# Attention with a routed expert layer in one kernel: the first weight split a step earlier, counts for the second token list later, one transposition and one small load moved

## The chip, the cores and the metric

The kernel runs on one core of a Trainium2 chip. The metric is device time in microseconds (us) of one execution; lower is better. Engines have short names here: PE is TensorE (matmuls; PEld its weight loads), DVE VectorE, ACT ScalarE, POOL GpSimd, SP SyncE, whose queue issues most DMAs. Each engine works through its own instructions strictly in the order in which the program was written.

## What is computed

Attention over 8 batches, 8 heads, 576 positions, width 64, in which keys and values are first condensed into 32 memory rows by a softmax over `phi`; its 4608 x 512 result goes through a layer of 8 experts, of which each token takes one.

```python
a = softmax(phi, over the 32 memory rows)
k_m = einsum('bhsm,bhsd->bhmd', a, k);  v_m = einsum('bhsm,bhsd->bhmd', a, v)
attn = softmax(q @ k_m^T / 8)
x = (attn @ v_m)                      # as 4608 tokens x 512
e = argmax(x @ w_gate)                # one expert for each token
gate = softmax(x @ w_gate)[e];  eom = sigmoid(x @ w_output_gate)[e]
out = gate * eom * (relu(x @ w1[e]) @ w2[e])
```

## The kernel before

**Attention.** The 8 batches are worked in 4 pairs (`NBP`). For a pair, `memory` turns the softmaxed `phi` (`turn_a`), sums keys and values into memory rows (`sums`), scales them (`spread`), turns `k_m` for use as weights (`turn_kv`) and multiplies `v_m` with both gate matrices, the tile `wg` (`gates`, copied by `gates2`). The order of these small steps is the tuple `MEM` (first pair: `MEM0`), in which "." gives control back. A pair has five steps `t` of the main loop `attention`; each runs through the list `ORDER`: `C` makes scores, `S` subtracts the largest, `X` takes exponentials, `D` and `B` divide and transpose, `V0` and `V1` multiply with the values, `M` and `m` advance `memory`, `R` advances the routing. The attended rows are stored to `xs` in DRAM.

**Routing.** After each pair, `rank` finds each token's expert and place. Token lists are made three times: list a behind the second pair and list b behind the third (both `route_early`), and list l behind the last (`route_late`). Each starts with `counts`, one matmul on `ohc` into the PSUM tile `pr`, and ends with index tiles `idx_...`, by which POOL gathers token rows (`xg`).

**Experts.** The work is cut into slots of 1 to 3 blocks of 128 tokens of one expert; two slots take list a, three take list b, the others list l. A slot has 8 weight units of 128 x 1024. Each comes by a DMA on SP's queue (`w`, buffers of the ring `raw`) and is split into a high and a low part: a cast on ACT and a subtraction on DVE into a tile `whl` of the ring `ring`. The first four units give 24 matmuls each (L1176), the last four 18 (L1198, three blocks). `turn_x` transposes the next slot's tokens on PE (L1041) while the present one runs.

**How the two meet.** The main loop runs alone up to item `S` of step `START` = 17, where it yields "open". From there on the expert code leads: `hook` is called every 6 or 12 expert matmuls and advances the attention loop by three items and the routing by two. `hold(n)` lets a routing step wait until `n` items have passed, but only once "open" has been yielded. `split(2)` under item `W` splits the first two weight units; `grow` at the end of step 16 adds buffers to `raw` and `ring` in the space that the attention inputs used.

Of the kernel before, what the change touches and what calls it, by code (L numbers as in the profile page):

```python
# [17 lines left out]
B, H, S, D, M = 8, 8, 576, 64, 32  # L18
# [14 lines left out]
NSLOT = NPE + NPT + NPP + NSS  # L33
NTHR = 13

ORDER = ["R4", "W", "X", "S", "R0", "m", "D", "M", "B", "V0", "R1", "R1", "V1", "M", "m", "C"]
LAG = {"X": 1, "B": 2, "D": 1, "V": 3, "C": -1}
TICK = 0
HOOK = (3, 2)
START = 17  # L40
# [3 lines left out]
NRAW = 3  # L44
NRING = 2
NLD = 2
MEM = ("a8", "a0", ".", "a2", ".", ".", "s0", ".", "a4", "s2", "x", "x", ".", ".", "s8", ".", "p0", "a6", ".", "x", ".", "s4", "x", "t0", ".", ".", "s9", "g0", "v0", ".", "s6", ".", "x", ".", "p1", "x", "t1", ".", ".", ".", "g1", "v1", ".")
MEM0 = ("a0", "s0", ".", "a2", "a8", ".", "s2", ".", "s8", "p0", "a4", ".", ".", "t0", ".", "g0", "a6", ".", "v0", "s9", "s4", ".", "s6", ".", ".", "p1", ".", "t1", "x", "x", ".", "g1", "x", ".", "v1", "x", ".", "x", ".", "x", ".", ".")
AWP = 1
NPK = 1  # L50
# [2 lines left out]
LATE = {"lg": 8, "w": 2, "pe": 3, "dve": 2}  # L53
# [13 lines left out]
def attention_moe(tc, phiT, kv, qT, wgo, wall, out):  # L67
    nc = tc.nc
    V, A, G, T = nc.vector, nc.scalar, nc.gpsimd, nc.tensor

    with contextlib.ExitStack() as ctx:
# [84 lines left out]
        G.affine_select(out=upto[:], in_=upto[:], pattern=[[1, E], [-1, E]], base=0,  # L156
                        channel_multiplier=0, compare_op=ALU.is_ge, fill=0.0)
        wg = cp.tile([P, H, 16], F32, name="wg")
        nc.sync.dma_start(wg[64:128], wgo)

        ohg = rt.tile([P, NCHT, E], BF16, name="ohg", bufs=1)
        jg = rt.tile([P, NCHT], I32, name="jg", bufs=1)
# [118 lines left out]
        def route_early(k):  # L281

            nm, n, s0, nch = "ab"[k], NPS[k], sum(NPS[:k]), (k + 2) * NCH
            eo, en = epcs[k], epcs[k + 1]
            yield from take_pr()
            yield from hold(LATE["pe"])
            n_ = counts(k + 1)
            yield
            yield from hold(LATE["dve"])
            fi = rt.tile([P, 1, E], F32, name="fi")  # L290
            ge = triples(fi[:, 0], n_, thr_e)
            next(ge)
            taken.clear()
            yield
            yield from ge
            V.scalar_tensor_tensor(fi[:, 0], fi[:, 0], 3.0, eo[:], ALU.mult, ALU.subtract)
            yield
            inc = (yield from prefix(fi[:], 1))[:, 0]
            exc = rt.tile([P, E], F32, name="exc")
            ie = rt.tile([P, E], F32, name="ie")  # L300
            V.tensor_scalar(ie[:], inc, 3.0 * n, None, ALU.min)
            V.tensor_tensor(exc[:], inc, fi[:, 0], ALU.subtract)
            yield
            V.tensor_scalar(exc[:], exc[:], 3.0 * n, None, ALU.min)
            cle = count_le(slot[:, s0:s0 + n], iota_3[:, 0:n], n, ie[:])
            next(cle)
            yield
            next(cle)
            V.tensor_tensor(ie[:], ie[:], exc[:], ALU.subtract)
            yield  # L310
            last(cle)
            V.tensor_tensor(en[:], eo[:], ie[:], ALU.add)
            V.tensor_tensor(exc[:], exc[:], eo[:], ALU.subtract)
            known(*order[s0:s0 + n])
            yield
            if k == 0:
                yield from hold(LATE["w"])
                stream.fetch()
            t1, t2, t3 = yield from lookup(nch, exc[:], en[:], eo[:])
            while k + 1 not in ranked:  # L320
                yield
            j = jg[:, 0:nch]
            V.scalar_tensor_tensor(t1, t1, 1.0, j, ALU.add, ALU.add)
            V.tensor_tensor(t2, j, t2, ALU.is_lt)
            V.tensor_tensor(t3, j, t3, ALU.is_ge)
            yield
            V.tensor_tensor(t1, t1, t2, ALU.mult)
            yield
            V.tensor_tensor(t1, t1, t3, ALU.mult)
            yield  # L330
            yield from table(nm, t1, nch, 3 * n)
            for z in order[s0:s0 + n]:
                z["listed"] = True
            if k == 0:
                gathers(0)
            yield
# [125 lines left out]
        def hold(n):  # L462

            if "open" not in env:
                return
            end = clock[0] + n
            while clock[0] < end:
                yield
# [115 lines left out]
        stream = Stream(0, NPE + NPT + NPP)  # L584
# [42 lines left out]
        def load_phi(bp):  # L627
            ph = ld.tile([P, 4, S], F32, name="ph")
            src = phiT[bp].rearrange("p (x s) -> p x s", s=S)
            for i in ((0, 2, 1, 3) if bp == 0 else (None,)):  # L630
                if i is None:
                    nc.sync.dma_start(ph[:], src)
                else:
                    nc.sync.dma_start(ph[:, i], src[:, i])
            phs[bp] = ph
# [14 lines left out]
        def loads():  # L650

            load_phi(0)
            for bp in range(NBP):
                for c in (0, 2, 4, 6):
                    load_kv(bp, c)
                    load_kv(bp, c + 1)
                    if bp == 0 and c == 2:
                        load_kv(0, 8)
                        load_q(0)
                        load_q(1)  # L660
                    if bp == 0 and c == PHI1:
                        load_phi(1)
                    if bp == 0 and c == 6:
                        for n in range(2, NQ):
                            load_q(n)
                    yield
# [399 lines left out]
        def attention():  # L1066

            nonlocal rou
            st, lgs = {}, {}
            while 0 not in kTs:  # L1070
                mem.step()
            st[0] = scores(0, 0)
            load_q(NQ)
            xo = None
            for t in range(NT + LAG["V"]):
                for w in ORDER:
                    g = t - LAG.get(w[0], 0)
                    if w in ("M", "m"):
                        if w == "M" or t % 5 < 4:
                            mem.step()  # L1080
                    elif w[0] == "R":

                        if len(left) < NBP - 1:
                            rou.step(int(w[1:]) * (2 if len(left) == 2 else 1))
                    elif w == "W":

                        while t == START and stream.split(2):
                            pass
                    elif w == "V0" and 0 <= g < NT:
                        bp, c = g // 5, g % 5  # L1090
                        while 2 * bp + (c >= 2) not in ves:
                            mem.step()
                        if g == 5 * bp:
                            lgs[bp] = rt.tile([P, NCH, 16], F32, name="lg", bufs=2)
                        xo = wk.tile([P, 2, 2, 2 * XQ], F32, name="xo", bufs=2)
                        values(bp, 2 * c, st[g], xo)
                    elif w == "V1" and 0 <= g < NT:
                        if c < 4:
                            values(bp, 2 * c + 1, st[g], xo)
                        store(bp, c, xo, lgs[bp])  # L1100
                    elif w == "C" and 0 < g < NT:
                        while 2 * (g // 5) + (g % 5 >= 2) not in kTs:
                            mem.step()
                        st[g] = scores(g // 5, g % 5)
                        if g + NQ < NT:
                            load_q(g + NQ)
                    elif w == "S" and 0 <= g < NT:
                        shift(st[g])
                    elif w == "X" and 0 <= g < NT:
                        expo(st[g])  # L1110
                    elif w == "D" and 0 <= g < NT:
                        divide(st[g])
                    elif w == "B" and 0 <= g < NT:
                        back(st[g])
                    undefer()
                    clock[0] += 1
                    yield "open" if w == "S" and t == START else None
                g = t - LAG["V"]
                if g >= 0 and g % 5 == 4:
                    bp = g // 5  # L1120
                    undefer(99)
                    left.append(bp)
                    rou.finish()
                    if bp < NBP - 1:
                        rou = Side(rank(bp, lgs[bp]))
                    else:
                        late.gens.append(rank(bp, lgs[bp]))
                if t == START - 1:
                    mem.finish()
                    pl.close()  # L1130
                    grow(0)
                if t == NT - 2:
                    pm.close()
# [232 lines left out]
```

## Time and profile before

| | |
|---|---|
| three runs | 577.61, 578.09, 582.82 us; median 578.09 us |
| the profiled execution | 577.36 us, of which the span of its instructions is 575.6 us |
| PE busy | 529.1 us, 92% of the span |
| DVE, ACT, POOL busy | 356.1, 280.4, 229.2 us |
| mean granted PE clock | 0.966 of full speed |

The times of rows count from the span's start. A timeline row is: start, duration, engine, line and operation, output<-inputs, shape, how many were merged, and in brackets the idle time of the engine just before with what ended it. The clock that PE was granted is given as a share of full speed: 1.00 is 2.4 GHz and 0.50 is 1.2 GHz.

### The profile page before, as it was taken

Reading aid. Unit: us, or ns where it says so; the run is one execution under the profiler, and the core shown is the slowest. Engines: PE = TensorE matmul, PEld = TensorE weight load, DVE = VectorE, ACT = ScalarE, POOL = GpSimd, SP = SyncE. Lnnn points to the kernel's source line nnn. Section 1 sums busy time; section 2 is a strip of 40 time slices with the busy share of each in tenths; the row PEclk is TensorE's granted clock in tenths of the full one; section 3 lists DMA queues with packets and bytes.
Section 4 is the critical chain, followed back from the end, with each engine's and each line's share of the span. In section 5 each row is a group of like instructions: output and inputs, shape, how many; then the busy total and the mean of one; then the engine's idle time right before and its main releaser. Section 6 shows DMA issues by size and latency. Waiting matters only on the chain. (4 is left out here: it accounts for less than half of the span.)

```text
span 575.6 us, 10886 instructions
## 1 busy us (share of the span) xinstructions
PE 529.1 (92%) x4031; PEld 455.6 (79%) x4031; DVE 356.1 (62%) x736; ACT 280.4 (49%) x496; POOL 229.2 (40%) x253
## 2 busy tenths in 40 slices
PE   3688886789899999999999999999999999999993
PEld 2455554478689799898998989898998989899893
DVE  4485979767765659996443555646465555676610
ACT  3475655454254456453434545445454445656510
POOL 2242575831166034312471735547170604553011
PEclk9987879989899999999999999999999999999998
DMA  8999999975367659756564665656465655687000
GB/s 308 413 401 391 382 376 356 308 301 168 116 197 245 209 173 308 246 155 183 161 200 145 204 177 180 184 171 176 139 202 168 179 172 181 198 264 223 7 28 32
DMA packets 42238, 124.14 MB, mean 216 GB/s; under 512 B 10368, under 2 KB 10432, under 8 KB 41792
## 3 DMA queue, kind: packets, MB, share of 16 engines
q1 hardware_dynamic: 35136, 102.71, 54.7%
q0 software_dynamic: 7040, 20.65, 10.4%
q8 instruction: 33, 0.54, 0.4%
q14 instruction: 29, 0.24, 0.1%
HBM read 102.99 MB, written 20.87 MB: 215 GB/s over the span
## 5 line engine op out<-in xcount | busy, mean ns | idle before, releaser
L1176 PE MATMUL bps<-xh,whl 128*128 128x384 f32 (+1 forms) x896 | 213.6, 322 | 0.1
L1198 PE MATMUL bps<-whl,hh 128*128 128x512 f32 x608 | 197.7, 396 | 0.0
L565 DVE TENSOR_TENSOR whl<-w,whl 128x1024 fp32r<-128x1024 f32 x112 | 136.8, 1228 | 68.5 <-ACT whl L564 68.5
L1176 PEld LDWEIGHTS bps<-xh,whl 128*128 128x128 f32 x896 | 156.9, 190 | 1.9 <-issue 0.6
L1176 PE MATMUL bps<-xl,whl 128*128 128x384 f32 (+1 forms) x448 | 143.8, 321 | 0.0
L1198 PEld LDWEIGHTS bps<-whl,hh 128*128 128x128 f32 x608 | 114.7, 189 | 26.1 <-issue 2.5
L1198 PE MATMUL bps<-whl,hl 128*128 128x512 f32 x304 | 119.0, 391 | 0.0
L564 ACT CAST whl<-w 128x1024 fp32r<-128x1024 f32 x112 | 116.4, 1046 | 0.0
L519 POOL DMA_INDIRECT xg<-xs,idx_ql x80 | 90.2, 1127 | 25.2 <-issue 24.3
L1181 ACT ACTIVATE hh<-bps 128x384 fp32r<-128x384 f32 (+1 forms) x96 | 48.9, 510 | 96.9 <-PE bps L1176 96.7
L1182 DVE SCALAR_TENSOR_TENSOR hl<-bps,hh 128x384 fp32r<-128x384 f32 (+1 forms) x96 | 55.1, 577 | 52.1 <-ACT hh L1181 52.1
L1176 PEld LDWEIGHTS bps<-xl,whl 128*128 128x128 f32 x448 | 85.1, 190 | 0.5
L1156 POOL DMA_INDIRECT out<-y,idx_ol x23 | 24.9, 1081 | 127.1 <-ACT y L1155 101.4
L1198 PEld LDWEIGHTS bps<-whl,hl 128*128 128x128 f32 x304 | 57.5, 189 | 10.8
L838 POOL TENSOR_TENSOR ea<-ea,mx 128x512 f32<-128x512 f32 (+1 forms) x20 | 19.2, 961 | 49.8 <-DVE mx L836 45.4
L1043 ACT CAST xh<-xt 128x384 fp32r<-128x384 f32 (+1 forms) x32 | 14.7, 460 | 37.9 <-DVE xt L1035 37.9
L873 ACT COPY xo<-bpd 128x576 f32<-128x576 f32 x36 | 22.6, 640 | 21.3 <-PE bpd L871 12.7
L956 POOL TENSOR_SCALAR Aw<-iota_row,row 128x128 bf16<-128x128 bf16 x36 | 26.8, 759 | 12.4 <-DVE row L946 12.4
L871 PE MATMUL bpd<-ve_b,aT 64*128 64x144 f32 (+1 forms) x320 | 28.5, 327 | 2.4 <-DVE ea L833 2.4
L1044 DVE TENSOR_TENSOR xl<-xt,xh 128x384 fp32r<-128x384 f32 (+1 forms) x32 | 15.8, 492 | 24.1 <-ACT xh L1043 24.1
L1155 ACT ACTIVATE y<-bps,gx 128x512 f32<-128x512 f32 x20 | 13.4, 687 | 30.4 <-PE bps L1198 13.9
L871 PEld LDWEIGHTS bpd<-ve_b,aT 64*128 64x128 f32 (+1 forms) x320 | 21.7, 196 | 8.1 <-issue 3.5
(248 smaller groups left out, 471.6 us busy)
## 6 DMA issues: line engine op xcount, KB each, us to landing
w<-wall SPq DMA_DIRECT2D x112, 512.0 KB, 3.9
kvt<-kv SPq DMA_DIRECT2D x32, 512.0 KB, 7.5
xs<-xo SPq DMA_DIRECT2D x16, 576.0 KB, 5.8
qt<-qT SPq DMA_DIRECT2D x16, 512.0 KB, 9.1
ph<-phiT SPq DMA_DIRECT2D x3, 1152.0 KB, 12.1
kv<-kv SPq DMA_DIRECT2D x4, 512.0 KB, 9.0
xg<-xs,idx_ql POOLq DMA_INDIRECT x80, 4.2
ph<-phiT SPq DMA_DIRECT2D x4, 288.0 KB, 3.2
```

Of the source, the lines that this page charges most:

```text
L519: G.indirect_dma_start(out=z["xg"][:, k, XQ * b:XQ * b + XQ], out_offset=None, in_=xs[0:z["rows"]].rearrange("t (a q) -> (t a) q", a=4), i ...
L564: A.copy(hl[:, 0], w[:])
L565: V.tensor_tensor(hl[:, 1], w[:], hl[:, 0].bitcast(F32), ALU.subtract)
L838: G.tensor_tensor(eav, eav, mx[:, 0:n].unsqueeze(2).to_broadcast([P, n, M]), ALU.subtract)
L871: T.matmul(px[to:to + n, r, sl], z["aT"][h, o:o + n], ves[2 * bp + b][h, g], start=True, stop=True)
L873: A.copy(xo[:, c % 2], px[:, :, 0:2 * XQ])
L956: (G if AWP else V).tensor_scalar(Aw[:, bp * NCH + c], iota_row[:], row[:, c:c + 1], None, ALU.is_equal)
L1156: G.indirect_dma_start(out=out, out_offset=bass.IndirectOffsetOnAxis(ap=z["idx"][1][:, z["q0"] + k:z["q0"] + k + 1], axis=0), in_=y[:], in ...
L1176: T.matmul(pb[:, j % pb.shape[1], 0:n_], w[:, b, o:o + P], x[a][:, cc, 0:n_], start=(n == 0), stop=(n == 11))
L1181: A.activation(h_[:, js, 0:n_], pb[:, :, 0:n_], AF.Relu)
L1182: V.scalar_tensor_tensor(l_[:, js, 0:n_], pb[:, :, 0:n_], 0.0, h_[:, js, 0:n_].bitcast(F32), ALU.max, ALU.subtract)
L1198: T.matmul(py[k], h[u - 4][a][:, f, k * P:(k + 1) * P], w[:, b, DM * f:DM * f + DM], start=(u == 4 and f == 0 and n == 0), stop=(u == 7 an ...
```

## The change

Four edits: item `W` leaves its place ahead of `X` for one between the last `M` and `m`, and its condition asks for step 16 instead of 17; in `MEM` the second turning of `k_m` ("t1") trades places with the pause behind it; `route_early` holds 6 items instead of 3 ahead of its counts; the load of `wg` is issued behind the four loads of the first `phi` instead of ahead of them.

```diff
-ORDER = ["R4", "W", "X", "S", "R0", "m", "D", "M", "B", "V0", "R1", "R1", "V1", "M", "m", "C"]
+ORDER = ["R4", "X", "S", "R0", "m", "D", "M", "B", "V0", "R1", "R1", "V1", "M", "W", "m", "C"]
...
-MEM = (... "p1", "x", "t1", ".", ".", ".", "g1", "v1", ".")
+MEM = (... "p1", "x", ".", "t1", ".", ".", "g1", "v1", ".")
...
         wg = cp.tile([P, H, 16], F32, name="wg")
-        nc.sync.dma_start(wg[64:128], wgo)
...
             yield from take_pr()
-            yield from hold(LATE["pe"])
+            yield from hold(2 * LATE["pe"])
             n_ = counts(k + 1)
...
             load_phi(0)
+            nc.sync.dma_start(wg[64:128], wgo)
             for bp in range(NBP):
...
                     elif w == "W":
-                        while t == START and stream.split(2):
+                        while t == START - 1 and stream.split(2):
                             pass
```

The edit of `MEM` moves no instruction on any engine: nothing else is written between its old and its new place. The other three do. Behind the edited lines, line numbers of the changed kernel are smaller by one.

**The counts for list b, on PE and on DVE.** On PE, during the first slot, before:

```order
L871 MATMUL bpd<-ve_b,aT 128x144 x4
L278 LDWEIGHTS ones_b
L278 MATMUL pr<-ohc_91,ones_b 128x8
L1198 MATMUL bps<-whl,hh 128x512
L1198 MATMUL bps<-whl,hl 128x512
L1198 MATMUL bps<-whl,hh 128x512 x2
L1198 MATMUL bps<-whl,hl 128x512
L1198 MATMUL bps<-whl,hh 128x512
L825 MATMUL bpd<-qt,kT_203 32x64 x8
L825 MATMUL bpd<-qt,kT_204 32x64 x8
L1041 MATMUL bps<-ident,xg 128x128 x3
```

The same stretch of PE in the changed kernel:

```order
L871 MATMUL bpd<-ve_b,aT 128x144 x4
L1198 MATMUL bps<-whl,hh 128x512
L1198 MATMUL bps<-whl,hl 128x512
L1198 MATMUL bps<-whl,hh 128x512 x2
L1198 MATMUL bps<-whl,hl 128x512
L1198 MATMUL bps<-whl,hh 128x512
L825 MATMUL bpd<-qt,kT_202 32x64 x8
L825 MATMUL bpd<-qt,kT_203 32x64 x8
L277 LDWEIGHTS ones_b
L277 MATMUL pr<-ohc_91,ones_b 128x8
L1041 MATMUL bps<-ident,xg 128x128 x3
```

The counts now stand behind six expert matmuls and the sixteen score matmuls. On DVE, the producer of `ohc` and the first reader of the counts (L192, in the changed kernel L191), before:

```order
L913 TENSOR_TENSOR ohc_91<-ohc_90,oc 128x8
L916 TENSOR_REDUCE zs<-w__2080 128x9
L192 TENSOR_TENSOR tge<-pr,thr_e 128x104
L194 TENSOR_REDUCE fi<-tge 128x8
L1044 TENSOR_TENSOR xl<-bps,xh 128x384
L833 STREAM_TRANSPOSE ea<-bpd 128x256
L836 TENSOR_REDUCE mx<-ea 128x8
L990 TENSOR_REDUCE lg<-xo 128x32
```

And in the changed kernel:

```order
L913 TENSOR_TENSOR ohc_91<-ohc_90,oc 128x8
L916 TENSOR_REDUCE zs<-w__2080 128x9
L1044 TENSOR_TENSOR xl<-bps,xh 128x384
L833 STREAM_TRANSPOSE ea<-bpd 128x256
L836 TENSOR_REDUCE mx<-ea 128x8
L990 TENSOR_REDUCE lg<-xo 128x32
L191 TENSOR_TENSOR tge<-pr,thr_e 128x104
L193 TENSOR_REDUCE fi<-tge 128x8
```

The writer of `ohc` keeps its place; the reader of the counts now stands behind four operations of attention and expert work.

**The first two splits, on DVE at the end of the attention part.** Before:

```order
L852 RECIPROCAL sa<-sa 128x16
L858 STREAM_TRANSPOSE aT<-ea 128x256
L779 COPY ve_b<-bpa 128x2x16
L565 TENSOR_TENSOR whl<-w,whl 128x1024 x2
L833 STREAM_TRANSPOSE ea<-bpd 128x512
```

And in the changed kernel:

```order
L852 RECIPROCAL sa<-sa 128x16
L858 STREAM_TRANSPOSE aT<-ea 128x256
L564 TENSOR_TENSOR whl<-w,whl 128x1024 x2
L779 COPY ve_b<-bpa 128x2x16
L833 STREAM_TRANSPOSE ea<-bpd 128x512
```

The two subtractions now stand ahead of one small copy; on ACT the two casts keep their place among the same neighbours.

**The index tiles of list b, on DVE during the second slot.** Before:

```order
L990 TENSOR_REDUCE lg<-xo 128x32
L242 CAST hl_i<-pr 128x2x9
L244 SCALAR_TENSOR_TENSOR iv<-hl_i 128x9
L1182 SCALAR_TENSOR_TENSOR hl<-bps,hh 128x384
L858 STREAM_TRANSPOSE aT<-ea 128x256
L249 TENSOR_SCALAR idx_gb<-iv 128x9
L250 TENSOR_SCALAR i_2548<-iv 128x9
L252 SCALAR_TENSOR_TENSOR idx_ob<-iv,i_2548 128x9
```

And in the changed kernel:

```order
L990 TENSOR_REDUCE lg<-xo 128x32
L1182 SCALAR_TENSOR_TENSOR hl<-bps,hh 128x384
L858 STREAM_TRANSPOSE aT<-ea 128x256
L241 CAST hl_i<-pr 128x2x9
L243 SCALAR_TENSOR_TENSOR iv<-hl_i 128x9
L1182 SCALAR_TENSOR_TENSOR hl<-bps,hh 128x384
L564 TENSOR_TENSOR whl<-w,whl 128x1024
L248 TENSOR_SCALAR idx_gb<-iv 128x9
L249 TENSOR_SCALAR i_2567<-iv 128x9
L251 SCALAR_TENSOR_TENSOR idx_ob<-iv,i_2567 128x9
```

The indices come one L1182 and one weight subtraction later than before.

## Rows read from the trace of the kernel before

**Rows 1.** The page's part 2, the span in 40 slices of 14.4 us

```profile
PE   3688886789899999999999999999999999999993
PEclk9987879989899999999999999999999999999998
DMA  8999999975367659756564665656465655687000
```

**Rows 2.** Waits of PE from 85 to 170 us: total us, times, longest

```profile
PE pr L278 <- DVE ohc L913: 3.9, 2, 2.4
```

**Rows 3.** Timeline from the start, SP's queue and DVE

```profile
0.80 0.59 SPq L159 DMA_DIRECT2D wg<-wgo  x1
...
1.44 1.99 SPq L634 DMA_DIRECT2D ph<-phiT  x4
...
6.45 2.67 DVE L677 TENSOR_REDUCE nmx<-ph 128x1 f32<-128x576 f32 x4
```

**Rows 4.** Timeline at the first splits

```profile
114.68 0.19 DVE L779 COPY ve_b<-bpa 128x32 f32<-128x32 f32 x1 [0.95 <-PE bpa L774]
...
115.93 2.36 DVE L565 TENSOR_TENSOR whl<-w,whl 128x1024 fp32r<-128x1024 f32 x2 [1.05 <-ACT whl L564]
...
118.20 0.71 DVE L833 STREAM_TRANSPOSE ea<-bpd 128x512 f32<-128x512 f32 x1
...
118.97 1.41 PE L1041 MATMUL bps<-ident,xg 128*128 128x128 f32 x9 [1.87 <-DVE ea L833]
```

**Rows 5.** Timeline around the counts for list b

```profile
142.55 0.76 PE L871 MATMUL bpd<-ve_b,aT 64*128 64x144 f32 x8
...
145.46 0.16 DVE L913 TENSOR_TENSOR ohc<-ohc,oc 128x8 bf16<-128x8 bf16 x1
...
145.68 0.17 PE L278 MATMUL pr<-ohc,ones_b 128*128 128x8 bf16 x1 [2.37 <-DVE ohc L913]
...
145.70 0.47 PE L1198 MATMUL bps<-whl,hh 128*128 128x512 f32 x1
...
145.88 0.27 DVE L192 TENSOR_TENSOR tge<-pr,thr_e 128x104 f32<-128x104 f32 x1
...
147.32 0.68 PE L825 MATMUL bpd<-qt,kT 64*32 64x64 f32 x32
...
147.93 0.90 PE L1041 MATMUL bps<-ident,xg 128*128 128x128 f32 x3
...
149.38 0.56 DVE L1044 TENSOR_TENSOR xl<-bps,xh 128x384 fp32r<-128x384 f32 x1 [2.94 <-ACT xh L1043]
...
150.66 0.37 DVE L990 TENSOR_REDUCE lg<-xo 128x32 f32<-128x128 f32 x1
...
150.90 0.21 PE L924 MATMUL pr<-ohg,strict 128*128 128x72 bf16 x1
```

**Rows 6.** Windows: stretch, its length, busy of each engine, granted PE clock, DMA share, GB/s

```profile
114.00:116.00 2.00, 2.00 (x38) 0.73 (x34) 0.27 (x2) 2.00 (x4) 0.55 (x1) 0.50 1.02 408
...
147.00:148.00 1.00, 1.00 (x35) 0.51 (x34) 0.00 (x0) 0.00 (x0) 0.00 (x0) 0.57 0.40 94
148.00:149.00 1.00, 1.00 (x4) 0.96 (x5) 0.00 (x0) 0.13 (x1) 0.00 (x0) 0.50 0.87 317
...
150.00:151.00 1.00, 1.00 (x7) 0.64 (x6) 0.97 (x4) 0.91 (x1) 0.11 (x1) 0.72 0.54 212
```

**Rows 7.** Timeline from list b to the transpositions for the third slot

```profile
177.57 0.17 DVE L252 SCALAR_TENSOR_TENSOR idx_ob<-iv,i 128x9 int32<-128x9 f32 x1
...
178.96 1.23 DVE L565 TENSOR_TENSOR whl<-w,whl 128x1024 fp32r<-128x1024 f32 x1 [0.38 <-ACT whl L564]
...
181.38 1.00 POOL L525 DMA_INDIRECT xg<-xs,idx_gb  x1 [0.30 <-issue]
...
191.04 0.49 PE L1041 MATMUL bps<-ident,xg 128*128 128x128 f32 x3
```

**Rows 8.** Gathers by lists a and b (L525) from 100 to 200 us

```profile
DMA to landing us min/median/max: 3.8/6.0/8.1
```

More of the change, by code (lines that the diff above doesn't have):

```diff
@@ L46 @@
 NLD = 2
-MEM = ("a8", "a0", ".", "a2", ".", ".", "s0", ".", "a4", "s2", "x", "x", ".", ".", "s8", ".", "p0", "a6", ".", "x", ".", "s4", "x", "t0", ".", ".", "s9", "g0", "v0", ".", "s6", ".", "x", ".", "p1", "x", "t1", ".", ".", ".", "g1", "v1", ".")
+MEM = ("a8", "a0", ".", "a2", ".", ".", "s0", ".", "a4", "s2", "x", "x", ".", ".", "s8", ".", "p0", "a6", ".", "x", ".", "s4", "x", "t0", ".", ".", "s9", "g0", "v0", ".", "s6", ".", "x", ".", "p1", "x", ".", "t1", ".", ".", "g1", "v1", ".")
 MEM0 = ("a0", "s0", ".", "a2", "a8", ".", "s2", ".", "s8", "p0", "a4", ".", ".", "t0", ".", "g0", "a6", ".", "v0", "s9", "s4", ".", "s6", ".", ".", "p1", ".", "t1", "x", "x", ".", "g1", "x", ".", "v1", "x", ".", "x", ".", "x", ".", ".")
```

## The prediction

> **What bounds the kernel now.** I read the page's slices first, by row: they split the span in two. Up to about 115 us the DMA engines stand at 9 in every slice but the first, and PE between 3 and 8; from about 160 us PE stands at 9 to the end of its work [rows 1]. So the first part is set by how early its bytes are moved, the second by PE alone, and a change can only pay where the loads begin, where one part hands over to the other, or where PE still waits behind that. The digits show such a place: the eleventh slice of PE, 144 to 158 us, is lower than those around it, though expert work is under way. The list of PE's waits names the cause: the counts matmul L278 waits for DVE's `ohc` [rows 2], and of its two waits the longer, 2.37 us, stands in the timeline at 145.68 [rows 5]. The windows show what follows: right behind the wait the clock of PE falls to about half, 0.57, 0.50 and 0.72 of full speed from 147 on (the window from 149 reads as the one from 148) [rows 6]. After 160 us there is nothing for this change to win, as PE never stands still; there the question is only what it may spoil.
>
> **The counts behind six expert matmuls.** The PE timeline [rows 5] gives the sum. PE is free at 142.55 + 0.76 = 143.31 and stands until 145.68. In the changed order it first does the six L1198, which took 145.70 to 147.32 = 1.62 us, and the scores L825, 147.32 to 147.93 = 0.61 us: 143.31 + 1.62 + 0.61 = 145.54. Its counts then need `ohc`, which DVE finishes at 145.46 + 0.16 = 145.62, since nothing ahead of L913 on DVE has changed. So they run at about 145.7 still, with a wait of 0.1 to 0.2 us, and the transpositions L1041 start at about 145.9 instead of 147.93: 2.0 us.
>
> Then the clock. From 147.93 to 150.90 PE did the three transpositions (0.90 us) and six L1198 at a lowered clock. At full speed the six take the 1.62 us seen above, and half of 0.90 is 0.45: 2.07 in place of 2.97, another 0.9 us. That the clock stays up is my reading of the rows: it was also at 0.50 at 114 us [rows 6], behind the slices in which PE is at 6 and 7, and its digits are 9 throughout where PE's are [rows 1]. If the wait goes and the clock with it, this edit is worth 2.9 us. Upwards it is bounded by the whole wait and the whole shortfall of the clock in those four windows: 2.37 + 0.43 + 0.50 + 0.50 + 0.28 = 4.1 us. Downwards by nothing gained, if the wait appears elsewhere.
>
> The Trainium skill (TensorE: Matmul & The Clock Gate, Part 1: The HAM clock gate) says that what watches PE's activity runs free of the kernel, so that the same kernel meets the change of clock at other matmuls in other runs. By that the 0.9 us would be a property of this one execution, and the edit would be worth 2.0 us.
>
> What is next late? Three places. First L924, which needs the PSUM tile that L192 has read, and L192 now stands behind L1044, L833, L836 and L990 on DVE. From L1041 to L1044 it took 149.38 - 147.93 = 1.45 us, from L1044 to the end of L990 151.03 - 149.38 = 1.65, L192 itself 0.27 [rows 5]: it ends at 145.9 + 3.4 = 149.3. PE has 0.45 of transpositions and now twelve L1198 (3.24 us) ahead of L924 and gets there at 149.6: covered by 0.3 us. Without that cover, PE pays what L192 is late, a few tenths.
>
> Second, list b. In the changed order its indices come behind one L1182 and the L565 which ends at 178.96 + 1.23 = 180.19; the last index operation then starts at about 180.45, an estimate, instead of 177.57: 2.9 us later against PE's own work [rows 7]. The third gather, issued at 181.38, would be issued at 184.3 and with the median landing of 6.0 us [rows 8] be there at 190.3, where PE turns the third slot's tokens at 191.04 [rows 7]. Both sides move earlier together if DVE keeps up with PE, which it can as its L1182 and L565 there wait for PE's and ACT's work. So it is hidden, by 0.7 us; at the longest landing of 8.1 it would cost 1.4 us.
>
> Third, weights. Units are split at PE's own pace, and when PE arrives earlier so do the requests; the subtraction that stands ahead of L913 on DVE is not moved. I take nothing for it.
>
> **The first weights.** The condition for `W` now holds at the end of step 16. On ACT nothing changes place, so the two casts start when they did; what moves is the pair of subtractions on DVE, ahead of the copy L779. That does not make them earlier: the first starts at 115.93, on a wait for ACT's cast, while L779 had been done in the idle time at 114.68 [rows 4]. It now lies between the pair and L833, and L833 is what the nine transpositions at 118.97 wait for. So this edit costs L779's 0.19 us at most; I take 0.15, bounds 0 and 0.19. The pair now uses the older buffers, and the next two weight loads on SP must wait for the two subtractions instead of going to new space; the stores and loads queued behind them on SP start later by the same. Their cover is that the second pair of units is cast only after PE has finished the first unit; nothing for it, and if it were gone, what they land late. Where `W` stood, the list is one item shorter and `m`, `C` and `R4` come one item later against the expert work, so that one set of scores comes half a unit of matmuls later and the third list's routing a hook later. PE does the same work in another order there: nothing.
>
> **The load of `wg`.** The four loads of `phi` start 1.44 - 0.80 = 0.64 us earlier [rows 3]. DVE's first reduction starts at 6.45 with no wait in front of it, right behind its own set-up work [rows 3], so the computing doesn't begin earlier. But the DMA engines are full from then on [rows 1], so all that is moved after it can be earlier by up to 0.64; `wg` itself is 64 rows and is wanted much later. I take 0.4 us, as toward 115 us DVE, ACT and POOL chains also set the pace; bounds 0 and 0.64.
>
> **The turning of `k_m`.** No instruction moves and none is added: 0.
>
> **Sum.** Against the profiled execution of 577.36 us: -0.4 + 0.15 - 2.9 = -3.15, so 574.2. The two close runs, 577.61 and 578.09, lie 0.5 above the profiled one on the mean, and 582.82 stands apart; I put the forecast at 574.5. A change of under 1%, 5.8 us, is about what a measurement of this kernel cannot tell from no change, and the forecast lies within it.
>
> **Rivals.** *The wait only moves.* DVE works in order, and its index and attention work for the next stage follows right there. If PE stands again at L924, or at the third slot's transpositions for 1.4 us (longest landing), with another lowered clock behind it, some 1.5 to 2.9 us are given back: 576 to 577.4. Against it stand the covers of 0.3 and 0.7 us worked out above; for it, that both are thin.
>
> *The clock does not follow.* Only the 2.0 us of the wait are won and PE meets a lowered clock somewhere else in that stage: 577.9 (the mean of the two close runs) - 0.25 - 2.0 = 575.6. The low windows right behind the wait speak against it. It is the outcome that the page of the Trainium skill named above suggests.
>
> *Everything is kept.* The start's 0.64 us reach the hand-over whole, the wait and the clock are won to their bound of 4.1, and L779 costs nothing: 577.9 - 4.7 = 573.2; and as the first part is a long chain of loads, stores and buffer releases, another timing of its DMAs can add a microsecond or two: down to 571.5.
>
> *Slower: list b decides.* If DVE does not follow PE forward between 150 and 180 us, the last index operation starts at 180.45 in absolute time, while PE arrives at 191.04 - 2.9 = 188.1. It decides from a start after 178.3 on (188.1 - 6.0 - 3.8, the 3.8 from index to third gather). At 180.45 PE stands 2.2 us at the median landing and 4.3 at the longest, and the clock falls behind it again, which cost 0.9: 5.2 us lost against 3.15 won, or 580.
>
> **How the numbers follow.** The forecast, 573.5 to 575.5, has 0.56; the wait that moves 0.16; the clock that doesn't follow 0.07; everything kept 0.15; slower by list b 0.06. The range 571.9 to 577.6 takes in nearly all of them but the last and leaves out somewhat under 2 in 10. Faster by over 1% needs under 572.3, the far half of the fourth case: 0.10. Slower by over 1% needs 583.9, beyond even the last case's 580: 0.02, and the rest, 0.88, is within 1%.
>
> **What would show it.** Right: PE's wait for `ohc` at 145 is under 0.3 us; the granted clock is 1.00 through 147 to 151; the nine transpositions for the first slot start within half a microsecond of 118.97 [rows 4]; PE's work is at 9 from 144 us on and ends about 3 us earlier. `phi`'s four loads are issued at 0.80, and L779 runs behind the two subtractions at about 118.3. Wrong: a new wait of PE for L191's tile, for a gather by list b near 188 us, or for a subtraction; or a hand-over that has moved by more than a microsecond in either direction, as the DMA-bound part then answers to its start otherwise than by a shift.

## The result and the profile after

The changed kernel takes 574.87 us (median of 14 runs, 573.17 to 577.51), the kernel before beside it 578.81 us (14 runs, 576.71 to 582.82): a ratio of 0.9931, 95% interval 0.9910 to 0.9951, or 4.0 us less, under 1%. The forecast was 574.5. The profiled execution of the changed kernel took 573.62 us with a span of 571.7, 3.9 less than the span of before.

The page's part 2 of the changed kernel, slices of 14.3 us, answers to [rows 1]:

```profile
PE   3788787779999999999999999999999999999993
PEclk9978988889999999999999999999999999999997
DMA  8999999975548668656574655656365655687000
```

The eleventh digit of PE is 9 now. The clock's digits in the first ten slices differ here and there from [rows 1] in both directions; from the eleventh on they are 9 in all but the last.

The timeline at the start, SP's queue and DVE, answers to [rows 3]. The loads of `phi` are issued at 0.80 in place of 1.44, and DVE's first reduction starts at 6.42 in place of 6.45, so nothing was won there, as worked out:

```profile
0.80 1.82 SPq L633 DMA_DIRECT2D ph<-phiT  x4
...
2.66 0.57 SPq L652 DMA_DIRECT2D wg<-wgo  x1
...
6.42 2.67 DVE L677 TENSOR_REDUCE nmx<-ph 128x1 f32<-128x576 f32 x4
```

The timeline at the first splits answers to [rows 4]. L779 stands behind the pair of subtractions, the casts still come 0.65 us behind the start of the gate matmuls L774 (113.43; before 0.64), and PE still waits for L833, 2.38 us in place of 1.87:

```profile
113.66 1.06 PE L825 MATMUL bpd<-qt,kT 64*32 64x256 f32 x12
...
114.08 1.99 ACT L563 CAST whl<-w 128x1024 fp32r<-128x1024 f32 x2
...
115.16 2.36 DVE L564 TENSOR_TENSOR whl<-w,whl 128x1024 fp32r<-128x1024 f32 x2 [2.68 <-ACT whl L563]
...
117.44 0.18 DVE L779 COPY ve_b<-bpa 128x32 f32<-128x32 f32 x1
117.54 0.70 DVE L833 STREAM_TRANSPOSE ea<-bpd 128x512 f32<-128x512 f32 x1
...
118.30 2.18 PE L1041 MATMUL bps<-ident,xg 128*128 128x128 f32 x9 [2.38 <-DVE ea L833]
```

The PE timeline around the counts for list b answers to [rows 5]. PE goes on from the attention matmuls L871 through six L1198 and the scores L825, and waits 0.39 us for the counts in place of 2.37:

```profile
141.56 0.76 PE L871 MATMUL bpd<-ve_b,aT 64*128 64x144 f32 x8
...
143.51 0.40 PE L1198 MATMUL bps<-whl,hh 128*128 128x512 f32 x1
143.84 0.46 PE L825 MATMUL bpd<-qt,kT 64*32 64x64 f32 x32
144.69 0.17 PE L277 MATMUL pr<-ohc,ones_b 128*128 128x8 bf16 x1 [0.39 <-DVE ohc L913]
144.71 0.53 PE L1041 MATMUL bps<-ident,xg 128*128 128x128 f32 x3
...
147.85 0.21 PE L924 MATMUL pr<-ohg,strict 128*128 128x72 bf16 x1
```

L924 has no wait in front of it. The windows of the changed kernel answer to [rows 6]; the third number from the right is the granted clock, which stays at 1.00 where it was 0.57, 0.50 and 0.72:

```profile
147.00:148.00 1.00, 1.00 (x10) 0.65 (x9) 0.96 (x5) 0.33 (x2) 0.62 (x1) 1.00 0.81 272
148.00:149.00 1.00, 1.00 (x15) 0.88 (x12) 1.00 (x2) 0.00 (x0) 0.00 (x0) 1.00 1.01 399
...
150.00:151.00 1.00, 1.00 (x13) 0.81 (x10) 0.96 (x5) 0.48 (x1) 0.72 (x1) 1.00 0.93 211
```

The timeline of list b answers to [rows 7]. The last index operation comes 1.1 us earlier than before, the third gather 2.1 us earlier, PE's transpositions for the third slot 4.4 us earlier, and there is still no wait in front of them:

```profile
176.44 0.17 DVE L251 SCALAR_TENSOR_TENSOR idx_ob<-iv,i 128x9 int32<-128x9 f32 x1
...
179.29 1.00 POOL L524 DMA_INDIRECT xg<-xs,idx_gb  x1 [0.30 <-issue]
...
186.60 0.49 PE L1041 MATMUL bps<-ident,xg 128*128 128x128 f32 x3
```

**Where the 3.9 us went.** I compared the first matmuls of the expert units in the two traces. The first unit starts at 120.14 (before 120.43), the second at 125.76 (126.75): 0.99 us are won at the hand-over, 0.70 of them inside the first unit, in which the clock is back at 1.00 from 122 us on (before from 124). From the fourth unit's start to the eighth's, the stretch that holds the counts, it took 22.49 us (135.03 to 157.52) in place of 25.95 (136.01 to 161.96): 3.46 us. From the 21st unit to the last matmul of the last unit it took 0.71 us more (344.30 against 343.59), 0.41 of which is one new wait, for the late list:

```profile
259.53 0.53 PE L234 MATMUL pr<-bwl,Aw 128*128 128x90 bf16 x9 [0.41 <-DVE bwl L226]
```

### The profile page after: what moved, and what is told of

It is laid out like the page before. It is cut to its first block, busy times and chain, and to the rows that moved or that the text cites. A ratio compares the mean times of both kernels' runs of the same rounds, so it can differ in the third digit from the quotient of the medians.

```text
span 571.7 us, 10886 instructions
## 1 busy us (share of the span) xinstructions
PE 528.8 (92%) x4031; PEld 456.4 (80%) x4031; DVE 353.9 (62%) x736; ACT 278.7 (49%) x496; POOL 228.2 (40%) x253
## 5 line engine op out<-in xcount | busy, mean ns | idle before, releaser
L1198 PE MATMUL bps<-whl,hh 128*128 128x512 f32 x608 | 197.3, 395 | 0.0
L1198 PEld LDWEIGHTS bps<-whl,hh 128*128 128x128 f32 x608 | 114.2, 188 | 23.7 <-issue 0.2
L1198 PE MATMUL bps<-whl,hl 128*128 128x512 f32 x304 | 118.7, 390 | 0.0
L1182 DVE SCALAR_TENSOR_TENSOR hl<-bps,hh 128x384 fp32r<-128x384 f32 (+1 forms) x96 | 55.0, 575 | 48.6 <-ACT hh L1181 48.4
L1198 PEld LDWEIGHTS bps<-whl,hl 128*128 128x128 f32 x304 | 57.2, 188 | 10.7
L871 PE MATMUL bpd<-ve_b,aT 64*128 64x144 f32 (+1 forms) x320 | 29.4, 332 | 2.9 <-DVE ea L833 2.9
L1155 ACT ACTIVATE y<-bps,xg 128x512 f32<-128x512 f32 x18 | 12.4, 688 | 38.2 <-DMA out<-y,idx_ob 10.2
L871 PEld LDWEIGHTS bpd<-ve_b,aT 64*128 64x128 f32 (+1 forms) x320 | 22.6, 203 | 8.7 <-issue 3.4
```

Source lines behind the costliest of these rows:

```text
L871: T.matmul(px[to:to + n, r, sl], z["aT"][h, o:o + n], ves[2 * bp + b][h, g], start=True, stop=True)
L1182: V.scalar_tensor_tensor(l_[:, js, 0:n_], pb[:, :, 0:n_], 0.0, h_[:, js, 0:n_].bitcast(F32), ALU.max, ALU.subtract)
L1198: T.matmul(py[k], h[u - 4][a][:, f, k * P:(k + 1) * P], w[:, b, DM * f:DM * f + DM], start=(u == 4 and f == 0 and n == 0), stop=(u == 7 an ...
```

## Experiments

Two questions were open: which of the edits carries the gain, and whether the lowered clock behind the wait belongs to the wait or to one execution. Twelve kernels were timed in three groups of four, each group on a chip of its own and beside runs of the kernel before, whose median there was 578.68, 579.29 and 578.28 us. The table gives for each the ratio to before, and from its profiled execution the time of the first expert matmul, PE's wait for the counts of list b, the lowest granted clock in the windows of 1 or 2 us behind it, and the time from the fourth unit's start to the eighth's ("stretch"). Kernels of different groups are compared by these ratios; "after, again" is the changed kernel timed once more.

| kernel | median us | ratio, 95% interval | first matmul | wait | clock | stretch |
|---|---|---|---|---|---|---|
| before | 578.81 | 1 | 120.43 | 2.37 | 0.50 | 25.95 |
| after | 574.87 | 0.9931, 0.9910 to 0.9951 | 120.14 | 0.39 | 1.00 | 22.49 |
| counts alone | 575.90 | 0.9962, 0.9946 to 0.9978 | 122.88 | 0.40 | 1.00 | 22.46 |
| first weights alone | 579.77 | 1.0015, 0.9998 to 1.0031 | 124.23 | 2.36 | 1.00 | 24.49 |
| `wg` alone | 577.16 | 0.9984, 0.9967 to 1.0001 | 120.58 | 2.36 | 1.00 | 24.48 |
| wait filled | 577.76 | 0.9985, 0.9963 to 1.0008 | 121.90 | filled | 1.00 | 24.47 |
| `k_m` alone | 579.34 | 0.9990, 0.9968 to 1.0013 | 122.25 | 2.36 | 0.50 | 25.96 |
| all but the counts | 579.78 | 1.0003, 0.9975 to 1.0030 | 120.69 | 2.36 | 1.00 | 24.47 |
| all but the first weights | 575.91 | 0.9949, 0.9926 to 0.9972 | 120.94 | 0.40 | 1.00 | 22.49 |
| after, again | 575.75 | 0.9954, 0.9921 to 0.9986 | 120.92 | 0.40 | 1.00 | 22.49 |
| weights ahead of `X` | 571.58 | 0.9881, 0.9855 to 0.9906 | 120.10 | 0.39 | 1.00 | 22.46 |
| counts at 9 items | 580.18 | 1.0037, 1.0019 to 1.0055 | 121.25 | 0 | 1.00 | 22.15 |
| counts at 12 items | 581.61 | 1.0048, 1.0030 to 1.0066 | 121.77 | 0 | 1.00 | 22.01 |
| counts at 0 items | 582.10 | 1.0065, 1.0040 to 1.0090 | 121.56 | 4.63 | 0.50 | 29.09 |

**The counts alone.** The kernel before with

```diff
-            yield from hold(LATE["pe"])
+            yield from hold(2 * LATE["pe"])
             n_ = counts(k + 1)
```

> The kernel before with the longer hold ahead of the early lists' counts alone. Theory A (the counts carry the gain): PE's wait for the counts falls from 2.37 us to under 0.5 us, the granted clock is 1.00 from 146 to 151 us, and the time falls by 2.9 to 3.7 us, a ratio of 0.9935 to 0.995. Rival B (the splits a step sooner carry it): the wait goes, but under 1 us is won in the time.

It gains 2.2 us (1.3 to 3.1), less than the 2.9 to 3.7 expected and more than the 1 us of the rival, and its wait is 0.40 us. Its profile shows something that I had not reckoned with: up to the hand-over its program is that of before, and yet its first expert matmul comes 2.4 us later. A single profile can't price an edit ahead of the hand-over.

**The first weights alone.** `W` behind the last `M`, asked for in step 16; the rest as before.

> The kernel before with the item W moved and its step changed, alone. Theory A: the casts keep their place, the nine transpositions for the first slot start within 0.3 us of 118.97, the wait for the counts stays at about 2.4 us; the time moves by 0 to +0.3 us. Rival B: the first expert matmul starts over 1 us earlier and 1.5 us or more is won.

It is 0.9 us slower, interval from 0.1 faster to 1.8 slower. The windows of its trace across the counts are the surprise:

```profile
149.00:150.00 1.00, 0.35 (x3) 0.31 (x3) 0.88 (x4) 0.00 (x0) 0.00 (x0) 1.00 0.00 0
150.00:151.00 1.00, 1.00 (x6) 0.74 (x4) 0.38 (x2) 0.00 (x0) 0.00 (x0) 1.00 0.89 82
151.00:152.00 1.00, 1.00 (x38) 0.68 (x36) 0.00 (x0) 0.00 (x0) 0.00 (x0) 1.00 0.58 139
```

PE stands for 2.36 us as in before, and the clock behind it stays at 1.00.

**The load of `wg` alone.** The load moved behind `load_phi(0)`.

> The kernel before with the load of wg behind the first phi, alone. Theory A: the first phi load is issued at 0.80 us, the transpositions for the first slot start 0.4 to 0.7 us earlier than 118.97, the time falls by as much. Rival C (the attention part answers to its start by more than a shift): they start over 1.5 us earlier or later.

It gains 0.9 us, interval from 1.9 faster to none. The wait is 2.36 and the clock behind it 1.00, as in the run before this.

**The wait filled.** The kernel before with 19 matmuls of 256 columns, whose result nobody reads, ahead of the counts for list b; they are additional work and stand in PE's idle time.

```diff
+            for i in range(1 + fill):      # fill is 19 for list b, else 0
+                T.matmul(... 128x256 bf16 ... if i < fill else counts ...)
...
-            n_ = counts(k + 1)
+            n_ = counts(k + 1, 19 * k)
```

> The kernel before with 19 extra matmuls of 128x256 (bf16, into the PSUM tile of the counts, overwritten by the counts; their result is used by nobody) put into the 2.37 us in which PE waits for the second early counts. The counts themselves start where they did, at about 145.7. Theory A (the lowered clock comes from the idle stretch): the clock stays at 1.00 from 146 to 151 us, and 0.9 to 1.8 us are won without any wait being removed. Rival D (the clock dips at this place whatever PE does): the dip stays, and the time is as before or up to 0.3 us longer.

The timeline of PE shows the time filled:

```profile
144.71 2.25 PE L279 MATMUL pr<-Aw,ones_b 128*128 128x256 bf16 x19
147.14 0.17 PE L279 MATMUL pr<-ohc,ones_b 128*128 128x8 bf16 x1 [0.19 <-DVE ohc L914]
```

The clock stays at 1.00, but the stretch takes 24.47 us, the same as in the two kernels above whose wait was not filled. So this run alone doesn't show that the filling held the clock up, and its median, 0.9 us less (2.1 less to 0.5 more), decides nothing.

**The turning of `k_m` alone.** "t1" and the pause behind it change places.

> The kernel before with the turning of k_m alone moved; its instructions stand in the same order on every engine. All theories expect no difference: ratio within 0.998 to 1.002. The profile serves as another execution of the order of before: if the hand-over is set by the order, the first expert unit starts at 120.4 us again, within 0.3; if it scatters by itself, it starts anywhere between 120 and 124. The wait for the counts stays at 2.4 us; by the theory that the lowered clock belongs to the wait, PE's clock is at half speed behind it again; by the theory that it belongs to single executions, it may stay at 1.00.

No instruction moves, and the ratio is 0.9990 with 1 well inside. The windows behind its wait of 2.36 us show the lowered clock of before again:

```profile
148.00:149.00 1.00, 1.00 (x4) 0.39 (x2) 0.00 (x0) 0.00 (x0) 0.00 (x0) 0.66 1.08 111
149.00:150.00 1.00, 1.00 (x35) 0.75 (x35) 0.00 (x0) 0.00 (x0) 0.00 (x0) 0.50 0.73 221
150.00:151.00 1.00, 1.00 (x5) 0.90 (x4) 0.00 (x0) 0.37 (x1) 0.00 (x0) 0.50 0.99 382
```

So of five profiled executions with the wait at 2.36 (the fifth is the next kernel below), two met the lowered clock and three did not, and it costs 25.95 - 24.48 = 1.47 us where it comes; none of these kernels was profiled more than once. Its first expert matmul at 122.25, against 120.43 in the same order of instructions, is the scatter of the hand-over once more.

**All but the counts.** `W`, "t1" and `wg` as in the changed kernel, the counts as before.

> The changed kernel with the counts back in their old place, so the first weights, the load of the gates' weights and the turning of k_m alone. Theory A (the edits add up: the counts' place 2.0 to 2.3 us, the gates' weights 0.4 to 0.9, the first weights within 0.3): -0.3 to -1.0 us against before, with the wait for the counts at 2.4 us. Theory B (the start's edits cancel, as the sum of the two alone did, -0.9 and +0.9): 0. Theory E (the first weights pay only together with the later counts): -0.2 to +0.5.

No difference: 0.2 us more, from 1.4 less to 1.7 more. The gain needs the counts. Its profiled execution lost 3.8 us between 400 and 416 us, in waits that no other trace has; how often its other runs met them is not on record, so its median may hold some of this.

**All but the first weights.** The counts, "t1" and `wg` as in the changed kernel, `W` as before.

> The changed kernel with the first weights back in their old step, so the later counts, the load of the gates' weights and the turning of k_m. Theory A (the edits add up, the first weights are worth within 0.3 us): -2.4 to -3.5 us against before and within 0.6 us of the changed kernel. Theory B (the first weights cost 0.9 us, as measured alone): -3 to -3.5, and as fast as the changed kernel or up to 0.9 us faster. Theory E (the first weights pay only together with the later counts): -2.2, some 1.5 us slower than the changed kernel.

It and the changed kernel, timed side by side, are 0.16 us apart (575.91 and 575.75, the changed kernel being the faster). Theory E, that the first weights pay only together with the counts, wanted 1.5 us between them, and the run of the first weights alone 0.9 the other way. Neither shows; but the intervals of the two ratios are 1.3 and 1.9 us to either side, so neither is excluded.

**The changed kernel again.**

> The changed kernel once more, beside its parts on the same chip. All theories expect -3 to -4 us against before (ratio 0.993 to 0.995); the wait for the counts at 0.4 us or less, and the clock at 1.00 behind it. If the first expert unit starts at another time than 120.1 us, by more than half a microsecond, the hand-over scatters from one execution to the next in this order too.

2.7 us less (0.8 to 4.6), below the 3 to 4 us expected at its middle. The first expert matmul is at 120.92, and PE has no wait for the late list.

**The first weights ahead of `X`.** The changed kernel with `W` in its old place in the list, but still in step 16.

```diff
-ORDER = ["R4", "X", "S", "R0", "m", "D", "M", "B", "V0", "R1", "R1", "V1", "M", "W", "m", "C"]
+ORDER = ["R4", "W", "X", "S", "R0", "m", "D", "M", "B", "V0", "R1", "R1", "V1", "M", "m", "C"]
```

> The changed kernel with the first weights split still earlier: W stands ahead of X within step 16, so that the casts stand ahead on ACT and fall into its idle time near 108 to 111 us. Theory A (no place of the first weights shows in the time, since the hand-over scatters by 2 us from one execution to the next whatever the order): within 0.6 us of the changed kernel, -2.4 to -4 against before. Theory W (the hand-over waits for the casts): the first expert unit starts 1 to 2 us earlier and the kernel is at 573, ratio 0.990. Theory X (the split delays the copy L833 on DVE, for which PE's transpositions wait): 1 to 3 us slower than the changed kernel.

571.58 us: 6.9 us less than before (5.4 to 8.4), and by the ratios 3 to 4 us less than the changed kernel, 574.87 and 575.75. This is the fastest version; I had only half expected it: theory W came nearest in time, but its sign, a first expert matmul 1 to 2 us earlier, is not in the trace. The timeline shows how it differs:

```profile
109.05 1.99 ACT L563 CAST whl<-w 128x1024 fp32r<-128x1024 f32 x2
...
110.13 4.09 DVE L564 TENSOR_TENSOR whl<-w,whl 128x1024 fp32r<-128x1024 f32 x2 [1.29 <-ACT whl L563]
...
116.10 1.06 PE L825 MATMUL bpd<-qt,kT 64*32 64x256 f32 x12
...
117.31 0.15 DVE L779 COPY ve_b<-bpa 128x32 f32<-128x32 f32 x1
117.49 0.72 DVE L833 STREAM_TRANSPOSE ea<-bpd 128x512 f32<-128x512 f32 x1
...
118.26 0.29 PEld L1041 LDWEIGHTS bps<-ident,xg 128*128 128x128 f32 x2 [0.43 <-DVE ea L833]
```

The casts come at 109.05 in place of 114.08, and the pair of subtractions with them, so that the pair no longer stands between the scores and L833. The wait of the weight loads (PEld) for L833 ahead of the nine transpositions, 1.6 to 2.9 us in the other thirteen traces, is 0.43 here. From the end of the last scores (116.10 + 1.06 = 117.16) to the first expert matmul it takes 2.94 us; in the trace of after 5.42, in the other thirteen 4.91 to 5.77. Some of this is paid earlier: the pair now stands ahead of the L833 before, for which PE waits 1.08 us at 114.91.

The first expert matmul comes no earlier than in the trace of after (120.10 and 120.14), as this execution had reached the last gate matmuls L774 2.4 us later (115.86 and 113.43), and with 573.14 us it was one of the two slowest of the six runs of this kernel. From the 21st unit to the end it takes 343.59 us as in before, where after takes 344.30. That the shorter way from the scores to the experts, with these 0.7 us, makes up the 3 to 4 us is argued, not shown: the spans of the two traces, 571.3 and 571.7 us, differ by 0.4.

**The counts one item group later.** The changed kernel with `hold(3 * LATE["pe"])`.

> The changed kernel with the counts of early lists one more unit's half later, behind twelve expert matmuls and three transpositions. The wait of 0.40 us for the counts goes. The last index operation of list b falls behind two more evictions on DVE, some 4.5 us later. If list b's cover is as thin as the prediction took it (0.7 us), PE waits 1 to 4 us for a gather ahead of the third slot near 187 us and the kernel is 1 to 3 us slower than the changed one, near 577 to 578; if the gathers still land in time, it is 0.4 us faster than the changed kernel.

The wait for the counts is gone and the stretch 0.34 us shorter, but the kernel is 2.1 us slower than before (1.1 to 3.2). The place is not the one I named. In the timeline, PE stands for the token list itself, ahead of list b's matmuls L234:

```profile
171.10 0.34 PE L1176 MATMUL bps<-xh,whl 128*128 128x384 f32 x1
175.12 0.87 PE L234 MATMUL pr<-bwb,Aw 128*128 128x18 bf16 x27 [3.68 <-DVE bwb L226]
```

and DVE, in order, has L226 behind a subtraction that waits for a cast of weights. On ACT this cast stands behind an operation that waits 6.80 us for a store of `out` by list a, 5.37 us in the trace of after, where L226 has already run:

```profile
171.08 0.69 ACT L1155 ACTIVATE y<-bps,xg 128x512 f32<-128x512 f32 x1 [6.80 <-DMA out<-y,idx_oa]
...
172.74 1.23 DVE L564 TENSOR_TENSOR whl<-w,whl 128x1024 fp32r<-128x1024 f32 x1 [7.32 <-ACT whl L563]
173.88 0.55 DVE L1182 SCALAR_TENSOR_TENSOR hl<-bps,hh 128x384 fp32r<-128x384 f32 x1
174.34 0.72 DVE L226 TENSOR_TENSOR bwb<-eq,tok_hl 128x243 bf16<-128x243 bf16 x2
```

A window shows the clock behind this wait:

```profile
174.00:178.00 4.00, 2.88 (x34) 2.88 (x34) 3.76 (x8) 0.80 (x2) 0.98 (x1) 0.62 0.70 214
```

From the eighth unit to the 21st it takes 66.31 us in place of 61.29: 3.68 of the 5.0 are the wait; the rest lies behind it, where the clock is down.

**The counts two groups later.** The changed kernel with `hold(4 * LATE["pe"])`.

> The changed kernel with the counts of early lists two steps later, behind eighteen expert matmuls. No wait for the counts. List b's indices fall behind three more evictions, some 6.7 us later, so PE should wait 3 to 6 us ahead of the third slot near 187 us, perhaps with a lowered clock behind it: 3 to 6 us slower than the changed kernel, 578 to 581. If there is no wait there, 0.4 us faster than the changed kernel, and the prediction's cover of 0.7 us was wrong.

2.8 us slower than before (1.7 to 3.8). Here the wait is the one that the prediction's last rival named, for a gather of list b ahead of the third slot:

```profile
184.01 1.06 POOL L524 DMA_INDIRECT xg<-xs,idx_gb  x1 [10.24 <-DVE idx_ob L251]
...
193.45 0.47 PE L1041 MATMUL bps<-ident,xg 128*128 128x128 f32 x1 [3.98 <-DMA xg<-xs,idx_gb]
193.58 0.78 PE L1198 MATMUL bps<-whl,hh 128*128 128x512 f32 x1
```

With 0.32 in front of it that is 4.3 us, and the window from 194 to 196 us shows the clock at 0.50 behind it; from the eighth unit to the 21st it takes 67.44 us, 6.15 more than after.

**The counts earlier.** The kernel before with `hold(0)`: the counts ahead of six expert and four attention matmuls that stand in front of them in before.

> The kernel before with the counts of early lists earlier instead of later: ahead of the six expert matmuls and of four attention matmuls that stand in front of them now. PE stands for ohc from about 141 us: the wait grows from 2.36 us by these six and four matmuls (1.62 + 0.76) to 4.7 us. By the wait alone: +2.4 us against before (581.5, ratio 1.004). By the theory that a wait of this length lets the clock fall in some executions and a longer one in more of them: up to 1.5 us on top, 582 to 583, with the clock at half speed behind the wait in the profile. If the time stays at that of before, the wait is not on the path at all.

582.10 us, 3.8 us more than before (2.3 to 5.2), and the wait is 4.63 us, 2.27 more. The windows:

```profile
143.00:147.00 4.00, 0.02 (x1) 0.00 (x0) 3.90 (x11) 0.66 (x2) 1.05 (x1) 0.79 0.03 12
147.00:149.00 2.00, 2.00 (x6) 1.56 (x6) 0.59 (x3) 0.00 (x0) 0.00 (x0) 0.50 0.46 109
149.00:151.00 2.00, 2.00 (x11) 1.25 (x9) 0.00 (x0) 0.00 (x0) 0.00 (x0) 0.50 0.38 154
151.00:153.00 2.00, 2.00 (x9) 1.40 (x6) 0.00 (x0) 0.64 (x1) 0.00 (x0) 0.71 0.07 25
```

The stretch is 29.09 us: 4.61 over the 24.48 of a wait of 2.36 with the clock up, 2.27 of it the wait and 2.34 the clock.

## Why the prediction was right

**The wait for the counts: right.** Predicted 2.0 us. The stretch takes 24.47 to 24.49 us with the old place and the clock up, and 22.46 to 22.49 with the new one, in five profiled executions: 2.0. What is left of the wait is 0.39 to 0.40 in place of the predicted 0.1 to 0.2. I took the scores L825 at 0.61 us from [rows 5], where the clock was already down [rows 6]; at full clock they take 0.46, and the six L1198 took 1.52 in place of 1.62 (142.32 to 143.84), so PE comes to the counts that much sooner.

**The clock: near in size, its cause not settled.** I took 0.9 us for it on the ground that it followed from the wait. Where the lowered clock comes it costs 1.47 us, but it came in only two of five executions with that wait. If that is its share, 2/5 of 1.47 is 0.6, and 2.0 + 0.6 = 2.6 us. The medians allow it: the four kernels with the later counts and the old or new first weights have a mean ratio of 0.9949, the four without them (the filled one left aside) 0.9998; the difference of 0.0049 is 2.8 us, against the 2.9 of the sum. From the intervals of the eight ratios I put it at 0.9 us to either side, so it does not tell whether the clock adds 0.6, 0.9 or nothing to the 2.0.

So the rival in which the clock is a matter of the execution has three traces on its side, whose clock stayed up behind the same wait. The Trainium skill (TensorE: Matmul & The Clock Gate, Part 1: The HAM clock gate) says that the same kernel meets the change of clock at other matmuls in other runs. The five traces fit that and do not prove it: the two with the lowered clock are the two whose instructions stand in the order of before, and each of the three others has an edit ahead of the hand-over, if in the `wg` kernel only one load near the start. What the rival had wrong is that the edit then meets the lowered clock somewhere else: in the five executions with the wait at 0.4 us the granted clock reads 1.00 from 128 to 560 us throughout.

**The first weights: right at the hand-over, wrong behind it.** Predicted +0.15. The casts kept their place, as worked out, and PE's wait for L833 behind the pair [rows 4] stayed. From the end of the last scores to the end of L833 it takes 3.39 us in before (114.41 + 1.11 = 115.52 to 118.91) and 3.52 in after; the medians of the seven traces with the old place and the six with the new one are 3.39 and 3.48, so 0.1. The medians of times, 0.16 us apart, resolve neither that nor its sign. What the moved item does to the order of the third list's routing was put at nothing, and there the traces say otherwise: in all six with the new place the 29th to 31st units take 0.13 to 0.71 us longer than in before, and the 15th to 18th 0.11 less, while in the seven with the old place and in the kernel that puts `W` ahead of `X` both take the same. The new wait of 0.41 us at L234 is part of this. What I saw in [rows 4] and did not follow up is that the pair itself, not L779, holds L833 back: where `W` stands ahead of `X`, L833 ends 1.05 us behind the scores.

**`wg` and `k_m`: not resolved.** Predicted -0.4 and 0. Alone they measure -0.9 (-1.9 to 0) and -0.6 (-1.9 to +0.8), all three edits without the counts +0.2 (-1.4 to +1.7). The 0.99 us that the profile of after wins at the hand-over is within the scatter of 2.4 us among executions of the same order, and is not put down to an edit.

**The covers: right, and thin.** L924 met no wait; L191 ended at 147.36 + 0.26 = 147.62, 0.23 us ahead of it, where 0.3 was worked out. The indices of list b came 3.3 us later against PE's own work (1.1 us earlier, while PE came 4.4 earlier), where 2.9 was worked out, and PE met no wait for its gathers. But one group of items later PE stands 3.68 us for the list and the whole gain is gone; so the rival that ends slower was a matter of one item group, at a place (L234) ahead of the gathers that I had watched.

**The number: in part luck.** That 574.87 lies so near to 574.5 hides two misses that cancel: the sum took 3.15 us from some 577.9, which is 574.7 and was put at 574.5, while the kernel before measured 578.81 beside the changed one, and the change was worth 4.0 us (2.8 to 5.2; 2.7 when timed again). I also held that a change of this size could hardly be told from none; 14 runs of each told it.

**Signs that failed.** The wait was to be under 0.3 us and is 0.39; the nine transpositions were to start within half a microsecond of 118.97 and started at 118.30. L779 ran at 117.44, not at 118.3.

## What to carry to other kernels

A wait of one matmul for a short chain on another engine is best removed by other matmuls that are ready, and the right amount is found by moving it both ways: here six matmuls earlier costs 3.8 us, six later gains 2.8 and twelve later loses it all, because the same step heads a list that is needed later. Ask of a step that is moved, but lands behind the same release, what stands behind it on its engine: the split seems to have paid only when it left the front of the copy that PE waited for. Price nothing ahead of a DMA-bound hand-over from one profile; take medians of parts side by side, and inside a fixed stretch compare the stretch.

## What was not expected of the hardware

The end of the part in which the DMA engines are full scatters between executions of the same instructions: the first expert matmul came at 120.43, 121.56, 121.90, 122.25 and 122.88 us in five traces whose instructions are the same up to there. They come from more than one chip; 121.90 and 122.88 are from the same one. Behind it the stretch of the table repeats to 0.03 us wherever the order and the clock are the same.

The clock fell behind a standing PE in some executions and not in others at a middle length of the wait: at waits of 0.39 to 0.40 us in none of five traces, at 2.36 in two of five, at 3.68, 3.98 and 4.63 in all three.
